# A two-layer MHA + S4D kernel on one core: block 30's sums by a product, a pool for the first-stage buffers, tied additions, a load told to the plan, end additions on VectorE

## The chip, the cores and the metric

The kernel runs on 1 core of one Trainium2 chip. TensorE is PE in the profile, VectorE DVE, ScalarE ACT, GpSimd POOL, SyncE SP; PEld is TensorE's weight load. The metric is the device time of one execution in microseconds, lower is better. Before the change it is 2667.18 us, the median of 3 runs between 2666.62 and 2667.36.

## The reference

A sequence x of 2048 rows and 640 channels passes through two layers, each of them an attention block and then an S4D convolution, each added to x:

```python
def _A_ref(x, wqkv, wo):                      # 32 heads of 20 channels
    ...
    scores = jnp.einsum("bhqd,bhkd->bhqk", q, k) * (Dh ** -0.5)
    p = _softmax(scores, axis=-1)
    o = jnp.einsum("bhqk,bhkd->bhqd", p, v)
    ...
def _B_ref(u, log_A_real, A_imag, C_real, C_imag, log_dt, D_skip):
    ...
    P = jnp.exp((A * dt[:, None])[:, :, None] * pos[None, None, :])
    K = 2.0 * jnp.einsum("dn,dnl->dl", C, P).real      # 128 states a channel
    Kf = jnp.fft.rfft(K, L2)
    Uf = jnp.fft.rfft(u_t, L2)
    y = jnp.fft.irfft(Uf * Kf[None, :, :], L2)[:, :, :L]
    ...
    return y + u * D_skip[None, None, :]
x = x + _A_ref(_layernorm(x, axis=-1), A_wqkv, A_wo)
x = x + _B_ref(_layernorm(x, axis=-1), B_log_A_real, ...)
x = x + _A_ref(_layernorm(x, axis=-1), A_wqkv, A_wo)
x = x + _B_ref(_layernorm(x, axis=-1), B_log_A_real, ...)
```

## The kernel before

**Stages.** In microseconds of the span: layer norm and first projections (0 to 116), attention 1 (to 1093), out-projection 1 with the transform of the S4D kernel (to 1272), S4D convolution 1 (to 1417), layer norm and projections of layer 2 (to 1486), attention 2 (to 2464), out-projection 2 (to 2509), convolution 2 (to the end).

**Attention** (`attention`). 32 blocks, each of 4 heads and 512 queries, run over 16 key tiles. `scores` multiplies S into PSUM (L866) and ACT exponentiates it into pt; `values` multiplies pt with V into pa (L900). V carries a column of ones, so pa also holds each query's sum. At the end of a block DVE adds the two halves of pa into oc, and the sums have to be inverted and spread over the 20 rows of their head. Two ways exist. The usual one goes through DRAM, each step appended to the list `later` with a due time: `sums` and `load` (dn, dr), `invert`, `back`, `spread` (db), and `scale`, which multiplies oc by db (L940) when the next block ends; all these DMAs are issued by POOL. The other, `at_once` (L882), is used for the last block alone: a product of oc with the constant matrix dsel puts each head's sum on all its rows (L886), then DVE does a maximum, a reciprocal and a multiply, and `store_block` stores oc. In layer 1 dsel is the tile late[0], which `prefetch` loads in the step `small` (L1183).

**What fills attention.** PE and DVE have other work laid between the exps: the projections of later heads (`jobs`, `qk`, the matmuls at L618 into PSUM tile m, evicted by DVE into qc) and in attention 1 the generator of the S4D kernel. That generator takes its powers from DRAM (`load_powers`, tile kpw, issued by POOL), and `expand` (L268) multiplies and copies them on DVE into tables, which `contract` multiplies on PE.

**The plan.** The order of each engine's instructions is written out when the program is built. `Plan` (L48) keeps an estimate of the time that PE, ACT and DVE have reached; each DVE operation adds to plan.dve (L80). Filler steps and the entries of `later` are laid where their due time lies by that estimate, and `emptied` lays evictions by it. `tie` (L93) makes an instruction stay behind another on the same engine without a semaphore. Operations of DVE, ACT, POOL and SP are recorded by a helper, so they all show line L78; they are told apart by their tiles.

**End of attention 1.** `prefetch` opens a pool on the memory that the generator has left, loads wo in five pieces (wot, split by POOL into woh and wol) and appends the loads of x, of the first S4D kernel block (kl) and of small tables. Blocks 30 and 31 are the last two (NBK is 32).

**Out-projection 1 and kernel transform.** `out_proj` multiplies po; after each 7th of its matmuls one step of `ktransform` is laid. For each of 5 channel blocks: `by_time` adds the skip weight to the first column of kl (L1250), transposes kl on PE (pkt) and evicts it as ktrh (ACT) and ktrl (DVE); `first_stage` multiplies it with the table e1s into pkx, evicted as x1; `turned` transposes that (pkt again) and evicts it as kxt, by ACT and DVE in turn (L1280); `ends` multiplies pkf, evicted as kn and stored into DRAM as kha and khb. The addition for block 0 is tied behind late[1], those of blocks 1 to 4 are not tied.

**Convolution** (`ssm`, L1385). 40 products of 128x512 (8 of each of 5 channel blocks). `stage1` multiplies the normalised rows uh, ul with e1s (psx, 2 buffers of x1, cast by ACT, rest by DVE); `stage2a` transposes and `sets` multiplies psx; `product` (L1459) shuffles psx on DVE into t, multiplies ka by psx on DVE, kb by t and adds the two on POOL (L1467) for all products but numbers 37 and 39, whose last two steps are on DVE; `stage3` multiplies the result with fa (psv), `stage4` with eb (psy), and DVE adds psy to x. The buffers: s1 (L1408) holds eb, ka, t2 and xt, s2 x1 and v. A pool's tiles may start only when every earlier tile on the same bytes has been released.

Of the kernel before, what the change touches and what calls it, by code (L numbers as in the profile page):

```python
# [87 lines left out]
def mha_s4d_kernel(ctx, tc, x_in, wqkv, wo, lar, aim, cr, ci, ldt, dsk,  # L88
# [109 lines left out]
    def kgen():  # L198
# [69 lines left out]
        def expand(k, w, tab, dif):  # L268

            while slow and slow[0][0] <= k:  # L270
                slow.pop(0)[1]()
            bs = slice(k * BC, k * BC + BC)
            lo = [tab[:, r, :, 0:24].rearrange("p d (g k) -> p d g k", k=8) for r in range(2)]
            hi = [tab[:, r, :, 24:28] for r in range(2)]
            for r in range(2):
                ve.tensor_mul(w[:, r], w[:, r], w[:, 2])
                a3 = w[:, r, 0:9, :].rearrange("p (g k) d -> p d g k", k=3)
                ve.tensor_copy(lo[r][:, :, :, 1:3], a3[:, :, :, 0:2])
                ve.tensor_copy(lo[r][:, :, :, 4:5], a3[:, :, :, 2:3])
                ve.tensor_copy(hi[r][:, :, 0:1], ld["ci" if r else "cr"][:, bs].unsqueeze(2))  # L280
                yield
            cm = [ld[n][:, bs].unsqueeze(2).to_broadcast([P, BC, 3]) for n in ("cr", "ci")]
            yield from cmul([a[:, :, 1:4] for a in hi], [w[:, r, 9:12, :].rearrange("p n d -> p d n") for r in range(2)], cm, [P, BC, 3], "kwc")
            yield from cmul([a[:, :, :, 3] for a in lo], [a[:, :, :, 1] for a in lo],
                            [a[:, :, :, 2] for a in lo], [P, BC, 3], "kwc")
            w4 = [a[:, :, :, 4:5].to_broadcast([P, BC, 3, 3]) for a in lo]
            yield from cmul([a[:, :, :, 5:8] for a in lo], [a[:, :, :, 1:4] for a in lo], w4, [P, BC, 3, 3], "kwb")
            ve.tensor_add(tab[:, 2], tab[:, 0], tab[:, 1])
            yield
            ve.tensor_sub(dif, lo[1][:, :, 0:3:2], lo[0][:, :, 0:3:2])  # L290
# [139 lines left out]
    def attention(x, stats):  # L430
# [461 lines left out]
        def values(qb, g, kt, pts, pa):  # L892
# [10 lines left out]
            if kt == NI - 1:  # L903
# [8 lines left out]
                sums_[0] = plan.dve + 0.15  # L912
                while scaled:
                    scaled.pop(0)()
                if blk == NBK - 1:
                    later.append((plan.dve, lambda: at_once(oc, blk)))
                    return

                def sums():
# [237 lines left out]
    def prefetch(x, rest):  # L1157
# [16 lines left out]
        if rest:  # L1174
# [2 lines left out]
                      *(w1.tile([P, NI, P], F16, name=f"ktr{n}") for n in "hl"),  # L1177
                      *(w1.tile([P, 4, 4, P], F32, name=f"kxt{n}") for n in range(2))]
            late[:] = [w1.tile([P, P], F32, name="dsel")]

            def small():
                sy.dma_start(kl0[1], dsk)
                sy.dma_start(late[0], c_dn)  # L1183
                sy.dma_start(kl0[2], c_f2.rearrange("p (s m) -> p s m", s=2))
            rest[1:1] = small, lambda: load_kl(0)
            with tc.tile_pool(name="wos", bufs=NCT, side="right") as ws:
# [54 lines left out]
    def ktransform(e1):  # L1241

        c = ExitStack()
        c2 = c.enter_context(tc.tile_pool(name="f2", bufs=2))
        kl, skip, f2, x1, hi, lo, *xts = kl0

        def by_time(b, h):

            if h == 0:
                tie(ve.tensor_add(kl[:, 0:1], kl[:, 0:1], skip[:, b:b + 1]), None if b else late[1])  # L1250
            klv = kl.rearrange("d (p i) -> d i p", i=NI)
            for i4 in (2 * h, 2 * h + 1):
                pt = pst("X", [P, 4, P], F32, tag="X", name="pkt")
# [18 lines left out]
        def block(b):  # L1272

            def turned(t, xt, h):
                for q in (2 * h, 2 * h + 1):
# [1 line left out]
                    for g in range(4):  # L1277
                        transpose(pt[:, g, :], of_group(x1, 16 * t + 4 * q + g), ident)
                    if q % 2:
                        ve.tensor_scalar_mul(xt[:, q], pt, ksc[:, 1:2])  # L1280
                    else:
                        se.activation(xt[:, q], pt, AF.Copy, scale=ksc[:, 1:2])

# [103 lines left out]
    def ssm(x, uh, ul, consts, last):  # L1387
# [18 lines left out]
        e1, f2, id16, fa = consts  # L1406
        with ExitStack() as c:
            c1 = c.enter_context(tc.tile_pool(name="s1", bufs=1))  # L1408
            c2 = c.enter_context(tc.tile_pool(name="s2", bufs=2))
            c3 = c.enter_context(tc.tile_pool(name="s3", bufs=3))  # L1410
            order = {}
# [38 lines left out]
                return px  # L1450

            def factors(m, ch):
                ka = c1.tile([P, 512], F32, bufs=5, name="ka")
                kb = c3.tile([P, 512], F32, name="kb")
                for t, src in ((ka, kha), (kb, khb)):
                    at("sp", sy.dma_start(t.rearrange("p (q k) -> p q k", k=P), src[m][:, ch]))
                return ka, kb

            def product(px, ka, kb, alone):  # L1459
                t2 = c1.tile([P, 512], F32, name="t2")  # L1460
                at("dve", ve.stream_shuffle(t2, px, SWAP))
                at("dve", ve.tensor_mul(ka, px, ka))
                for f, *a in (("tensor_mul", kb, t2, kb), ("tensor_add", ka, ka, kb)):
                    if alone:
                        at("dve", getattr(ve, f)(*a))
                    else:
                        at("pool", getattr(ge, f)(*a))  # L1467
                return ka

            def stage3(v, t, ch, t1):  # L1470
# [28 lines left out]
                return add, after  # L1499

            def new_x1():
                return [c2.tile([P, 4, NI // 2, 4, 32], F16, name=f"x1{k}") for k in range(2)]

            x1 = new_x1()
            for i2 in range(8):
                stage1(0, x1, i2)()
            ks, t1s, vs = {}, {}, {}
            NQ = 8 * NCT
            nxt, px = None, None
            sums = None  # L1510
            for n in range(NQ + 15):
# [3 lines left out]
                if n < NQ:  # L1515
                    if q == 0 and b:
                        x1 = nxt
                    if n % 4 == 0:
                        xt = c1.tile([P, 2, 4, 4, P], F16, name="xt")
                    stage2a(x1, q, xt)  # L1520
                if 2 <= n < NQ + 2:
                    ks[n - 2] = factors(*divmod(n - 2, 4))
                if sums:
                    sums[0]()
                if 4 <= n < NQ + 4:
                    t1s[n - 4] = product(px[n % 4], *ks.pop(n - 4), n > NQ and n % 2 == 1)
                if n < NQ and b + 1 < NCT:
                    if q == 0:
                        nxt = new_x1()
# [251 lines left out]
```

## Time and profile before

| | us |
|---|---|
| median of 3 runs | 2667.18 |
| profiled execution | 2665.94 |
| its span (first to last instruction) | 2664.1 |
| PE busy in the span | 2492.7 |
| ACT busy | 2342.6 |
| DVE busy | 1517.5 |
| POOL busy | 813.9 |
| mean granted TensorE clock | 0.993 |

A row of the instruction view shows the start in us from the span's beginning, the duration in us, engine, line, operation, the tile written and the tiles read, partitions x elements and type, and how many instructions like it followed each other. In brackets stand the idle time of that engine just before the row and what ended it: a tile written by another engine, or a DMA. A row whose second column is followed by DMA, or by an engine and a tile without an operation, is of the chain of waits that ended last: start, duration, what ran.

### The profile page before, as it was taken

The numbers are of one execution on the slowest core, as the hardware profiler recorded it, in microseconds if no ns is written. First come the engines' busy times: TensorE is split into PE (matmuls) and PEld (weight loads), VectorE is DVE, ScalarE is ACT, GpSimd is POOL, SyncE is SP. The second block draws the span as 40 slices with busy tenths as digits, with TensorE's granted clock in tenths as the row PEclk, the third lists the DMA queues.
The fourth block names the chain that finished last, engine by engine and source line by source line (L and its number), as shares of the span: only waits on it lengthen the run. The fifth ranks groups of instructions, "written<-read, shape, count | busy, mean of one in ns | idle before, by whom it ended". The sixth has DMA issues, their size and how long they took to land.

```text
span 2664.1 us, 118804 instructions
## 1 busy us (share of the span) xinstructions
PE 2492.7 (94%) x52388; PEld 1408.8 (53%) x52388; DVE 1517.5 (57%) x3417; ACT 2342.6 (88%) x2763; POOL 813.9 (31%) x1240
## 2 busy tenths in 40 slices
PE   7899999999999998799898999999999998999898
PEld 3445445444454443587796444454444443444798
DVE  7687778778855885376787333232232222143875
ACT  7899999999999999565765799999999999999474
POOL 1123334233332332311581122222222223222285
PEclk9999999999999999999999999999999999999999
DMA  6523222222222222454652121121121113222366
GB/s 208 185 52 85 60 78 71 77 57 74 56 60 51 51 69 76 168 204 164 213 175 72 41 58 51 50 60 47 43 67 38 51 32 91 69 67 57 124 201 183
DMA packets 186270, 241.99 MB, mean 91 GB/s; under 512 B 43408, under 2 KB 128720, under 8 KB 184080
## 3 DMA queue, kind: packets, MB, share of 16 engines
q1 hardware_dynamic: 150048, 188.28, 22.5%
q0 software_dynamic: 35696, 46.01, 7.4%
q8 instruction: 413, 6.77, 1.1%
q14 instruction: 113, 0.93, 0.1%
HBM read 158.16 MB, written 76.00 MB: 88 GB/s over the span
## 4 chain that ended last, share of the span: by engine, by line
ACT 58%; PE 19%; issue 10%; DVE 4%; DMA 4%; POOL 1%; SPq 0%; ACTq 0%; POOLq 0%; DVEq 0%
ACT pt L78 56%; PE psy L1417 3%; PE psv L1417 2%; PE pa L900 2%; PE po L193 2%; PE psx L1417 2%; PE S L866 1%; PE pst L1439 1%; PE pkx L193 1%; PE pkt L196 1%; PE m L618 1%; PE pq L771 1%; DVE x L78 1%; PE pkf L193 1%; DMA kl<-kd 0%
## 5 line engine op out<-in xcount | busy, mean ns | idle before, releaser
L78 ACT ACTIVATE pt<-S 128x1024 f32<-128x1024 f32 x2048 | 1927.3, 1033 | 32.9 <-PE S L866 20.3
L900 PE MATMUL pa<-pt,V 64*32 64x512 f32 x16384 | 1095.1, 590 | 0.2 <-DVE oc L78 0.2
L866 PE MATMUL S<-qop,kop 61*32 61x512 f16 x16384 | 874.7, 381 | 85.3 <-ACT pt L78 67.5
L866 PEld LDWEIGHTS <-kop 61*32 61x32 f16 x16384 | 365.8, 89 | 739.3 <-issue 620.1
L900 PEld LDWEIGHTS pa<-pt,V 64*32 64x32 f32 x16384 | 312.3, 106 | 68.6 <-issue 7.9
L78 POOL DMA_DIRECT2D dn<-oc x248 | 122.5, 501 | 595.3 <-DVE oc L78 575.8
L78 DVE TENSOR_SCALAR qc<-m 128x512 f32<-128x512 f32 (+1 forms) x68 | 46.8, 689 | 288.9 <-PE m L618 288.9
L78 POOL DMA_DIRECT2D db<-dn x248 | 125.1, 511 | 139.4 <-DMA dn<-dr 136.5
L78 DVE COPY oc<-pa 128x512 f32<-128x512 f32 x64 | 44.2, 691 | 195.1 <-PE pa L900 184.1
L78 POOL DMA_DIRECT2D ot<-oc x256 | 130.4, 516 | 81.2 <-DVE oc L78 53.8
L618 PE MATMUL m<-xh,wh 64*32 64x512 f16 x2560 | 144.4, 377 | 4.1 <-DVE qc L78 4.1
L618 PE MATMUL m<-xh,wl 64*32 64x512 f16 x2560 | 144.9, 377 | 0.0
L618 PE MATMUL m<-xl,wh 64*32 64x512 f16 x2560 | 143.5, 376 | 0.0
L78 ACT COPY xt<-pst 128x1024 f16<-128x1024 f16 x80 | 81.3, 1016 | 60.8 <-PE pst L1439 60.8
L618 PEld LDWEIGHTS <-wh 64*32 64x32 f16 x5120 | 90.4, 93 | 77.2 <-issue 34.6
L78 POOL DMA_DIRECT2D dn<-dr x62 | 34.5, 557 | 301.8 <-DVE dr L78 274.4
L1467 POOL TENSOR_TENSOR kb<-t,kb 128x512 f32<-128x512 f32 x76 | 97.2, 1279 | 66.8 <-DVE t L78 42.5
L78 DVE TENSOR_SCALAR V<-m 128x160 f32<-128x160 f32 x64 | 20.7, 324 | 161.8 <-PE m L584 161.8
L78 DVE TENSOR_TENSOR kb<-ktab 128x512 f32<-128x512 f32 x160 | 106.1, 682 | 0.0
L584 PEld LDWEIGHTS <-xh 128*128 128x128 f16 x960 | 79.4, 98 | 46.1 <-issue 30.3
L335 PEld LDWEIGHTS m<-kb,ka 128*32 128x32 f32 x3840 | 61.2, 110 | 74.1 <-issue 56.5
L1467 POOL TENSOR_TENSOR ka<-ka,kb 128x512 f32<-128x512 f32 x76 | 97.5, 1283 | 6.0
(312 smaller groups left out, 3945.1 us busy)
## 6 DMA issues: line engine op xcount, KB each, us to landing
ka<-kha SPq DMA_DIRECT2D x80, 256.0 KB
kb<-khb SPq DMA_DIRECT2D x80, 256.0 KB
db<-dn POOLq DMA_DIRECT2D x248, 64.0 KB, 3.3
kop<-ks SPq DMA_DIRECT2D x176, 80.0 KB
kpw<-wd POOLq DMA_DIRECT2D x60, 192.0 KB, 4.4
qop<-qs SPq DMA_DIRECT2D x256, 40.0 KB
ot<-oc POOLq DMA_DIRECT2D x256, 40.0 KB, 2.9
kha<-kn SPq DMA_DIRECT2D x20, 512.0 KB
```

Of the source, the lines that this page charges most:

```text
L78: made = f(out, *a, **k)
L193: chain(te.matmul(*a, **k))
L196: chain(te.transpose(*a, **k))
L335: chain(te.matmul(ps[32 * j:32 * j + 32, c8, :], a[n][:, ch, :], b[n][:, dd, :], start=(n == 0), stop=(n == 2), tile_position=(0, 32 * j)))
L584: chain(te.matmul(ps[:, :n], a_[:, ct, sl], m[:, ct, :], start=(k == 0), stop=(k == 14)))
L618: chain(te.matmul(ps[r][32 * t:32 * t + 32, :], a_[rows, ct, 32 * u:32 * u + 32], m[rows, ct, 512 * v:512 * v + 512], start=(k == 0), stop ...
L771: te.matmul(pq, a_[:, ct, :], m[:, ct, sl], start=(n == 0), stop=(n == 14))
L866: chain(te.matmul(S[32 * t:32 * t + 32, 512 * r:512 * r + 512], kt_[rows, kc + 32 * t:kc + 32 * t + 32], qt[rows, :], start=True, stop=Tru ...
L900: chain(te.matmul(pa[r][32 * j:32 * j + 32, :], V[rows, kt, VP * h:VP * h + 32], pts[j // 2][rows, 512 * (j % 2):512 * (j % 2) + 512], sta ...
L1417: at("pe", te.matmul(*a, **k))
L1439: at("pe", te.transpose(pt[:, k, g, :], of_group(x1[k], 4 * q + g), id16))
L1467: at("pool", getattr(ge, f)(*a))
```

## The change

It has five parts.

1. After the first multiply of the first expansion, plan.dve is raised by 6.0 us.
2. In layer 1 block 30 goes the way of block 31: its `at_once` is appended to `later` with a due time 6.0 us behind the block's end, and `later` is sorted. The load of dsel moves from `small` to the place where the tile is made, ahead of the loads of wo.
3. The addition of the skip weight is tied, for each channel block, behind the last eviction on DVE that `turned` has made (for the first block, as before, behind late[1]).
4. In the convolution x1 has a pool of its own, sx with 2 buffers, behind eb's; ka, t2 and xt move to a pool s4 behind that.
5. The last four products multiply kb on POOL and add on DVE, and each such addition is laid on DVE behind the shuffle and the multiply of the next product. Before, numbers 37 and 39 had both steps on DVE, 36 and 38 both on POOL.

```diff
--- before.py
+++ after.py
@@ -274,6 +274,8 @@
             hi = [tab[:, r, :, 24:28] for r in range(2)]
             for r in range(2):
                 ve.tensor_mul(w[:, r], w[:, r], w[:, 2])
+                if k == r == 0:
+                    plan.dve += 6.0
                 a3 = w[:, r, 0:9, :].rearrange("p (g k) d -> p d g k", k=3)
                 ve.tensor_copy(lo[r][:, :, :, 1:3], a3[:, :, :, 0:2])
                 ve.tensor_copy(lo[r][:, :, :, 4:5], a3[:, :, :, 2:3])
@@ -912,8 +914,9 @@
                 sums_[0] = plan.dve + 0.15
                 while scaled:
                     scaled.pop(0)()
-                if blk == NBK - 1:
-                    later.append((plan.dve, lambda: at_once(oc, blk)))
+                if blk == NBK - 1 or first_layer and blk == NBK - 2:
+                    later.append((plan.dve + (0.0 if blk == NBK - 1 else 6.0), lambda: at_once(oc, blk)))
+                    later.sort(key=lambda e: e[0])
                     return
 
                 def sums():
@@ -1177,10 +1180,10 @@
                       *(w1.tile([P, NI, P], F16, name=f"ktr{n}") for n in "hl"),
                       *(w1.tile([P, 4, 4, P], F32, name=f"kxt{n}") for n in range(2))]
             late[:] = [w1.tile([P, P], F32, name="dsel")]
+            sy.dma_start(late[0], c_dn)
 
             def small():
                 sy.dma_start(kl0[1], dsk)
-                sy.dma_start(late[0], c_dn)
                 sy.dma_start(kl0[2], c_f2.rearrange("p (s m) -> p s m", s=2))
             rest[1:1] = small, lambda: load_kl(0)
             with tc.tile_pool(name="wos", bufs=NCT, side="right") as ws:
@@ -1243,11 +1246,12 @@
         c = ExitStack()
         c2 = c.enter_context(tc.tile_pool(name="f2", bufs=2))
         kl, skip, f2, x1, hi, lo, *xts = kl0
+        hold = [late[1]]
 
         def by_time(b, h):
 
             if h == 0:
-                tie(ve.tensor_add(kl[:, 0:1], kl[:, 0:1], skip[:, b:b + 1]), None if b else late[1])
+                tie(ve.tensor_add(kl[:, 0:1], kl[:, 0:1], skip[:, b:b + 1]), hold[0])
             klv = kl.rearrange("d (p i) -> d i p", i=NI)
             for i4 in (2 * h, 2 * h + 1):
                 pt = pst("X", [P, 4, P], F32, tag="X", name="pkt")
@@ -1277,7 +1281,7 @@
                     for g in range(4):
                         transpose(pt[:, g, :], of_group(x1, 16 * t + 4 * q + g), ident)
                     if q % 2:
-                        ve.tensor_scalar_mul(xt[:, q], pt, ksc[:, 1:2])
+                        hold[0] = ve.tensor_scalar_mul(xt[:, q], pt, ksc[:, 1:2]).ins
                     else:
                         se.activation(xt[:, q], pt, AF.Copy, scale=ksc[:, 1:2])
 
@@ -1406,6 +1410,8 @@
         e1, f2, id16, fa = consts
         with ExitStack() as c:
             c1 = c.enter_context(tc.tile_pool(name="s1", bufs=1))
+            cx = c.enter_context(tc.tile_pool(name="sx", bufs=2))
+            c4 = c.enter_context(tc.tile_pool(name="s4", bufs=1))
             c2 = c.enter_context(tc.tile_pool(name="s2", bufs=2))
             c3 = c.enter_context(tc.tile_pool(name="s3", bufs=3))
             order = {}
@@ -1450,21 +1456,23 @@
                 return px
 
             def factors(m, ch):
-                ka = c1.tile([P, 512], F32, bufs=5, name="ka")
+                ka = c4.tile([P, 512], F32, bufs=5, name="ka")
                 kb = c3.tile([P, 512], F32, name="kb")
                 for t, src in ((ka, kha), (kb, khb)):
                     at("sp", sy.dma_start(t.rearrange("p (q k) -> p q k", k=P), src[m][:, ch]))
                 return ka, kb
 
             def product(px, ka, kb, alone):
-                t2 = c1.tile([P, 512], F32, name="t2")
+                t2 = c4.tile([P, 512], F32, name="t2")
                 at("dve", ve.stream_shuffle(t2, px, SWAP))
                 at("dve", ve.tensor_mul(ka, px, ka))
-                for f, *a in (("tensor_mul", kb, t2, kb), ("tensor_add", ka, ka, kb)):
-                    if alone:
-                        at("dve", getattr(ve, f)(*a))
-                    else:
-                        at("pool", getattr(ge, f)(*a))
+                at("pool", ge.tensor_mul(kb, t2, kb))
+                while adds:
+                    at("dve", ve.tensor_add(*adds.pop(0)))
+                if alone:
+                    adds.append((ka, ka, kb))
+                else:
+                    at("pool", ge.tensor_add(ka, ka, kb))
                 return ka
 
             def stage3(v, t, ch, t1):
@@ -1499,12 +1507,12 @@
                 return add, after
 
             def new_x1():
-                return [c2.tile([P, 4, NI // 2, 4, 32], F16, name=f"x1{k}") for k in range(2)]
+                return [cx.tile([P, 4, NI // 2, 4, 32], F16, name=f"x1{k}") for k in range(2)]
 
             x1 = new_x1()
             for i2 in range(8):
                 stage1(0, x1, i2)()
-            ks, t1s, vs = {}, {}, {}
+            ks, t1s, vs, adds = {}, {}, {}, []
             NQ = 8 * NCT
             nxt, px = None, None
             sums = None
@@ -1516,14 +1524,16 @@
                     if q == 0 and b:
                         x1 = nxt
                     if n % 4 == 0:
-                        xt = c1.tile([P, 2, 4, 4, P], F16, name="xt")
+                        xt = c4.tile([P, 2, 4, 4, P], F16, name="xt")
                     stage2a(x1, q, xt)
                 if 2 <= n < NQ + 2:
                     ks[n - 2] = factors(*divmod(n - 2, 4))
                 if sums:
                     sums[0]()
                 if 4 <= n < NQ + 4:
-                    t1s[n - 4] = product(px[n % 4], *ks.pop(n - 4), n > NQ and n % 2 == 1)
+                    t1s[n - 4] = product(px[n % 4], *ks.pop(n - 4), n >= NQ)
+                    if n == NQ + 3:
+                        at("dve", ve.tensor_add(*adds.pop(0)))
                 if n < NQ and b + 1 < NCT:
                     if q == 0:
                         nxt = new_x1()
```

## Prediction

> **What bounds the kernel now.** I read the page first, then busy times by stretch, then the instructions around the places that the diff touches.
>
> ```profile
> span 2664.1 us, 118804 instructions
> PE 2492.7 (94%) x52388; PEld 1408.8 (53%) x52388; DVE 1517.5 (57%) x3417; ACT 2342.6 (88%) x2763; POOL 813.9 (31%) x1240
> 360.00:1045.00 685.00, 656.86 (x17008) 312.94 (x17014) 519.77 (x1124) 676.93 (x721) 226.51 (x388) 1.00 0.25 62
> 1045.00:1110.00 65.00, 46.54 (x864) 21.37 (x848) 13.16 (x17) 50.32 (x57) 24.32 (x34) 0.95 0.58 198
> 1110.00:1280.00 170.00, 158.09 (x1891) 131.95 (x1892) 122.69 (x274) 94.70 (x158) 23.00 (x19) 0.98 0.49 175
> ```
>
> In the stretch rows the columns are length, then busy time of PE, PEld, DVE, ACT, POOL, granted clock, DMA share, GB/s. In attention 1 (360 to 1045) ACT works 676.9 of 685.0 us: its exps set the pace, and DVE has 165 us to spare. From 1045 to 1110, where attention gives way to the out-projection, nothing is full: PE 46.5 of 65, ACT 50.3, DVE 13.2. The out-projection with the kernel transform (1110 to 1280) is PE's, 158.1 of 170. So an edit pays only where ACT (attention) or PE (elsewhere) stands still. The profiled execution took 2665.94, 1.84 us more than its span and 1.24 under the median of 2667.18; I sum against 2665.94 and carry the difference to the median.
>
> **The plan's load (behind line 276): −5.5 us.**
>
> ```profile
> 123.54 0.56 DVE L78 TENSOR_TENSOR kpw<-kpw 128x384 f32<-128x384 f32 x1 [6.63 <-DMA kpw<-wd]
> 127.11 0.49 PE L618 MATMUL m<-xh,wl 64*32 64x512 f16 x8
> 133.99 0.68 DVE L78 TENSOR_SCALAR qc<-m 128x512 f32<-128x512 f32 x1
> 134.72 0.37 PE L618 MATMUL m<-xh,wh 64*32 64x512 f16 x1 [3.64 <-DVE qc L78]
> 137.43 1.02 ACT L78 ACTIVATE pt<-S 128x1024 f32<-128x1024 f32 x1 [5.13 <-PE S L866]
> 139.46 6.65 ACT L78 ACTIVATE pt<-S 128x1024 f32<-128x1024 f32 x7 [1.01 <-PE S L866]
> ```
>
> DVE waits 6.63 us for the first powers' load, works through their expansion (124.1 to 134.0, 9.9 us), and only then evicts the projection that PE had multiplied at 127.6. PE idles 3.64 us behind it, ACT 5.13 and then 1.01. The 6.0 us tell the plan of that wait, so it should lay the eviction behind at most half of the expansion: 124.1 + 9.9/2 = 129, five us earlier than now, more than PE's 3.64. The expansion that slides behind lies in DVE's spare time; without that cover its 9.9 us would be paid. But the plan's count shifts everything laid after it, so that another eviction can come late: bounds 0 and −6.1 (5.13 + 1.01). I take −5.5: the 5.13 and part of the 1.01.
>
> **The sums of block 30 (lines 915 and 1183): −6.5 us.**
>
> ```profile
> 1075.60 2.16 POOL L78 DMA_DIRECT2D dn<-oc  x4
> 1094.73 1.12 PE L886 MATMUL m<-oc,dsel 128*128 128x512 f32 x2 [0.46 <-DVE oc L78]
> 1096.55 1.26 ACT L78 ACTIVATE ktrh<-pkt,ksc 128x512 f16<-128x512 f32 x2
> 1103.61 0.69 DVE L78 TENSOR_TENSOR oc<-oc,db 128x512 f32<-128x512 f32 x1 [8.93 <-DMA db<-dn]
> 1104.22 0.74 DVE L78 SCALAR_TENSOR_TENSOR ktrl<-pkt,ksc,ktrh 128x512 f16<-128x512 f32 x1
> 1105.02 1.12 PE L196 MATMUL pkt<-ident,kl 128*128 128x128 f32 x4 [8.14 <-DVE ktrl L78]
> 1106.14 3.34 DVE L78 RECIPROCAL db<-db 128x512 f32<-128x512 f32 x1
> 1111.56 0.22 PE L193 MATMUL pkx<-ktrh,e1s 128*128 128x128 f16 x1 [2.57 <-DVE ktrl L78]
> 1096.00:1098.00 2.00, 0.87 (x7) 0.61 (x5) 0.00 (x0) 1.81 (x3) 0.76 (x2) 1.00 1.02 434
> 1102.00:1104.00 2.00, 0.00 (x0) 0.00 (x0) 0.39 (x1) 0.00 (x0) 0.00 (x0) 0.50 0.10 20
> ```
>
> Block 30's sums still go through DRAM, its stores issue only at 1075.6, and its inverse comes back behind loads that keep the DMA engines full (share 1.02 at 1096). DVE stands 8.93 us in front of line 940's scaling; queued behind it is ktrl, for which PE waits 8.14, and PE's clock then runs at 0.50 (1102 to 1104). With the product on PE its sums stay on the chip, without dn, dr or db transfers, and ktrl can go once ACT has written ktrh, at 1096.55 plus half of 1.26, so from about 1097.3. That is 1104.22 − 1097.3 = 6.9 us earlier, and pkx moves from 1111.56 to about 1104.7, just behind its e1s table: the DMA share is down to 0.10 at 1102, so the loads had landed by then. In exchange block 30 pays what block 31 pays: 1.12 us of PE, 0.7 max, 3.34 reciprocal, 0.7 multiply. DVE's three, 4.7 us, lie in the 51.8 idle us of 1045 to 1110; without that room the 3.34 would stand in front of block 31's copy of oc, for which the dsel product waits, and be paid. PE's 1.12 mostly fits its gaps between exps: +0.4. The dsel load, one issue of some 0.4 us, moves ahead of wo's on SP. If the loads bind instead, the 8.14 shrinks only by the removed transfers: bounds −2 to −7.5. I take −6.9 + 0.4 = −6.5.
>
> The Trainium skill (TensorE: Matmul & The Clock Gate, The HAM clock gate) says that after a few us of idleness PE is halved and needs about 3.4 us of work to be released. The trace agrees: 0.50 behind the 8.14 us. By it an idle time cut to under 3 us would also speed up the pkt and pkx behind it: some 4 us of work at half clock, an estimate of 2 us, and −8.5 for this part.
>
> **The tied additions (lines 1250 and 1280): −4.0 us.**
>
> ```profile
> 1145.13 0.16 DVE L78 TENSOR_TENSOR kl<-kl,skip 128x1 f32<-128x1 f32 x1 [2.08 <-DMA kl<-kd]
> 1175.81 0.92 DVE L78 TENSOR_TENSOR kl<-kl,skip 128x1 f32<-128x1 f32 x1 [1.14 <-DMA kl<-kd]
> 1209.47 0.16 DVE L78 TENSOR_TENSOR kl<-kl,skip 128x1 f32<-128x1 f32 x1 [3.87 <-DMA kl<-kd]
> 1210.08 0.70 PE L193 MATMUL po<-woh,ol 128*128 128x320 f32 x3 [2.93 <-DVE x L78]
> 1200.00:1220.00 20.00, 16.71 (x196) 13.10 (x195) 11.43 (x27) 8.97 (x16) 2.78 (x2) 0.91 0.63 217
> 1225.83 0.75 DVE L78 TENSOR_SCALAR kxt<-pkt,ksc 128x512 f32<-128x512 f32 x1 [0.43 <-PE pkt L196]
> 1226.82 0.90 PE pkt L196 x8
> ```
>
> DVE blocks on the next block's kl load three times (2.08, 1.14, 3.87); PE feels only the third: 2.93 us idle, and the stretch to 1220 has 3.3 us of idle and a clock of 0.91, which costs 20 × 0.09 = 1.8 more: 5.1. Tied behind the last turned eviction (1225.83 + 0.75 = 1226.6), the addition starts when PE reaches kl's transposes (1226.82), long after the load. Its 0.16 us then stands before PE in each of four blocks: up to +0.2 each, 0.8. Behind it on DVE are the evictions of po, for which PE's next po waits. −5.1 + 0.8 is −4.3; I take −4.0. If the tie makes PE wait for a whole round trip in each block, the bound is the dearest such stall seen, 5.1 each: −5.1 to −5.1 + 20.4 = +15.3.
>
> **Pools (lines 1408, 1454 and 1502): −0.8 us.**
>
> ```profile
> 1274.28 4.39 DMA khb<-kn
> 1275.78 0.56 ACT L78 CAST x<-psx 128x512 f16<-128x512 f32 x1
> 2513.14 0.56 ACT L78 CAST x<-psx 128x512 f16<-128x512 f32 x1
> L1417 PE MATMUL psx<-uhx,e1s x320: 216/219/314, 2474.9 to 2612.2; 128*128 128x128 f16 x160
> 2514.48 0.23 PE L1417 MATMUL psx<-uhx,e1s 128*128 128x128 f16 x1 [4.96 <-DVE va L78]
> ```
>
> A tile waits for every earlier tile that lay on its bytes. In layer 2 the first first-stage product ran at 2474.9, yet its cast at 2513.14: it shared bytes with wo's weights. In a pool of their own the x1 buffers lie on attention's, long free, so casts run beside the out-projection and PE's 4.96 us can go: 0 to −5, and I take −2.5, since the row names the LN's va as what PE waits for last. In layer 1, by tile sizes, the first x1 buffer now overlaps the second half of the transform's kn buffer, whose khb store lands 1274.28 + 4.39 = 1278.67: the cast at 1275.78 waits 2.9 us, and behind it on ACT the evictions that PE's next stage needs. 0 if PE has other work for as long, +3 if not; I take +1.7. Sum −0.8 (bounds −5 to +3).
>
> **Additions at the end (lines 1459–1468 and 1526): +4.0 us.**
>
> ```profile
> 1398.09 1.28 POOL L1467 TENSOR_TENSOR ka<-ka,kb 128x512 f32<-128x512 f32 x1
> 1398.05 0.73 DVE L78 STREAM_SHUFFLE t<-psx 128x512 f32<-128x512 f32 x1
> 1398.68 0.67 DVE L78 TENSOR_TENSOR ka<-psx,ka 128x512 f32<-128x512 f32 x1
> 1399.42 1.16 PE L1417 MATMUL psv<-fa,ka 128*128 128x128 f32 x8
> 1400.19 0.69 DVE L78 TENSOR_TENSOR ka<-ka,kb 128x512 f32<-128x512 f32 x1
> 2488.24 1.47 POOL L1231 TENSOR_TENSOR ulx<-u,uhx 128x640 f16<-128x640 f32 x1 [9.96 <-issue]
> 2488.55 1.18 DVE L78 TENSOR_TENSOR lt<-rs 128x2 f32<-128x2 f32 x1
> ```
>
> Product 36's addition ran on POOL until 1399.37, and psv followed at 1399.42. Now it runs on DVE behind the next shuffle and multiply: those end at 1399.35, plus 0.69, so psv starts at 1400.05: +0.6, for which I allow 0.9 in layer 2. Unblocked: +1.5. But a DVE operation on two SBUF tiles beside a POOL one can take longer: a 2-column lt took 1.18 us, to the end of POOL's ulx (2489.71), where the 1-column kl above took 0.16. So the addition would wait for POOL's multiply of product 37, which now follows the shuffle: 1398.78 + 1.28 = 1400.06, psv at 1400.75: +1.33, and with product 38's shuffle queued behind it, for which POOL waits in turn, about 0.5 for each of the next two: 2.4 a layer, +4.8. I take +4.0, near the blocked end.
>
> The Trainium skill (SBUF — State Buffer, Who interferes with whom) has it as a lock: a DVE instruction with two SBUF inputs waits out a GpSimd instruction that reads SBUF. It speaks against this edit. The trace agrees by the 1.18 us; by it the sum would be +4.8, without it +1.5.
>
> **Sum.** −5.5 − 6.5 − 4.0 − 0.8 + 4.0 = −12.8. The profiled execution goes to 2653.1, the median to 2667.18 − 12.8 = 2654.4.
>
> **Rivals.**
> 1. The plan's load only moves the stall: its count is wrong by as much elsewhere, another eviction meets another load. For it: DVE's order is fixed by an estimate of a load that took 6.63 us; against: DVE has room. −12.8 + 5.5 = −7.3: 2659.9.
> 2. The passage at 1100 is bound by loads, since the DMA engines are full from 1096 on. For: share 1.02; against: 0.10 at 1102, so the loads were over while DVE still waited. The sums' part falls from −6.5 to −2: 2658.9.
> 3. Slower: the tied addition becomes PE's wait. PE's order is chained; the addition follows the turned eviction, kl's transposes follow the addition, and PE has nothing laid between. From a round trip of about 3 us on, when the clock drops too, each of four blocks pays 5.1: the tie's −4.0 becomes +15.3, the sum −8.8 + 15.3 = +6.5, so 2673.7. Against: 0.16 us of addition, and only one eviction ahead.
> 4. The additions run unblocked, since the lt row is a single one (+1.5 for +4.0), and layer 2's casts save all 5 (−5 for −2.5): −12.8 − 5.0 = −17.8, so 2649.4. For: POOL and DVE share no row of this kind at the ends; against: the 1.18 ends when ulx does.
> 5. The change doesn't do what it says: the list of due times or the ties leave the order as it is. Nothing gained, nothing lost: 2667.
>
> **How the numbers follow.** Chances: forecast 0.47, rival 1 0.13, rival 2 0.12, rival 3 0.08, rival 4 0.12, rival 5 0.08. The likeliest case's own range is 2648 to 2660. The range 2644 to 2665 takes in rivals 1, 2 and 4 and most bounds (all at their low ends: −6.1 − 7.5 − 5.1 − 5 + 1.5 = −22.2, or 2645.0); rivals 3 and 5 are outside. A measurement of this kernel can tell 0.2%, 5.3 us: no change is 2661.8 to 2672.5. Faster: 0.46 of the forecast, 0.10 each of rivals 1 and 2, 0.12 of rival 4: 0.78. Same: 0.01, 0.03, 0.02 and 0.06 of these and rival 5: 0.12. Slower: rival 3 and 0.02 of rival 5: 0.10.
>
> **What would show it.** Plan: the exp wait of 5.13 us near 137 gone, and none of its size new before 400. Sums: no db wait over 2 us at 1095 to 1104, no half-clock stretch there, PE's 8.14 under 2. Tie: no kl wait on DVE, the stretch around 1200 to 1220 at clock 1.00; wrong if pkt waits for kl in every block. Pools: casts before 2500 in layer 2, a first cast after 1278 in shifted time in layer 1. Additions: psv waits for DVE instead of POOL at the ends, additions of 0.69 against up to 1.3 us. The forecast as a whole is wrong if the exps of attention lengthen, or a new wait of over 5 us on PE or ACT shows up in another place.

## The result and the profile after

The changed kernel takes 2674.44 us (median of 16 runs) against 2667.27 of the kernel before (16 runs): ratio 1.0027, interval 1.0019 to 1.0035. It is 7.2 us slower, where 12.8 less was forecast. The profiled execution took 2673.31, 1.13 under its median; its span is 2671.5, against 2664.1.

To see where it went, I took the same instruction (the n-th of its kind) in both traces, counted from 0. The last column is what the stretch above it added.

| instruction | before | after | lead (−) or lag | added |
|---|---|---|---|---|
| exp 0 | 116.03 | 114.60 | −1.43 | ahead of the change |
| exp 64 | 182.67 | 175.87 | −6.80 | −5.4 |
| exp 320 | 428.68 | 417.45 | −11.23 | −4.4 |
| exp 960 | 1032.81 | 1026.90 | −5.91 | +5.3 |
| first x += po | 1115.62 | 1116.60 | +0.98 | +6.9 |
| x += po 28 | 1257.84 | 1258.18 | +0.34 | −0.6 |
| first t of convolution 1 | 1290.95 | 1295.62 | +4.66 | +4.3 |
| x += psy 32 | 1410.89 | 1417.36 | +6.47 | +1.8 |
| exp 1984 | 2400.24 | 2408.33 | +8.09 | +1.6 |
| first t of convolution 2 | 2531.06 | 2537.95 | +6.89 | −1.2 |
| x += psy 72 | 2651.42 | 2658.77 | +7.35 | +0.5 |

The start gains what was forecast. Instruction rows of DVE in the changed kernel, with the columns as in the prediction:

```profile
122.03 0.56 DVE L78 TENSOR_TENSOR kpw<-kpw 128x384 f32<-128x384 f32 x1 [6.58 <-DMA kpw<-wd]
...
127.41 0.69 DVE L78 TENSOR_SCALAR qc<-m 128x512 f32<-128x512 f32 x1 [2.08 <-PE m L620]
```

The wait for the powers is still there (6.58), but the eviction now follows the product of PE (it waits for m, 2.08) and runs at 127.41 instead of 133.99. Then the end of attention 1. First the rows of POOL, SP and ACT, before:

```profile
1046.57 0.93 POOL L78 DMA_DIRECT2D kd<-ko  x1 [5.88 <-issue]
...
1074.10 1.55 POOL L1191 TENSOR_TENSOR wol<-wot,woh 128x640 fp32r<-128x640 f32 x1
1075.68 0.38 SPq L78 DMA_DIRECT2D otl<-ot  x1
1095.91 0.73 ACT L78 CAST oh<-otl 128x640 fp32r<-128x640 f32 x1 [3.87 <-DMA otl<-ot]
```

and after, with the rows of DVE, PE and ACT that follow from them:

```profile
1055.76 0.94 POOL L78 DMA_DIRECT2D kd<-ko  x1 [8.70 <-DVE ko L78]
...
1059.34 0.37 SPq L78 DMA_DIRECT2D dsel<-in_c_dn  x1
1060.06 2.27 SPq L78 DMA_DIRECT2D wot<-in_wo  x5
1061.30 2.05 PE L888 MATMUL m<-oc,dsel 128*128 128x512 f32 x2 [2.24 <-DMA dsel<-in_c_dn]
1064.04 1.02 ACT L78 ACTIVATE pt<-S 128x1024 f32<-128x1024 f32 x1 [3.61 <-PE S L868]
1073.75 3.05 POOL L1194 TENSOR_TENSOR wol<-wot,woh 128x640 fp32r<-128x640 f32 x2 [8.86 <-issue]
1082.52 1.55 POOL L1194 TENSOR_TENSOR wol<-wot,woh 128x640 fp32r<-128x640 f32 x1
1084.10 0.38 SPq L78 DMA_DIRECT2D otl<-ot  x1
1104.19 0.72 ACT L78 CAST oh<-otl 128x640 fp32r<-128x640 f32 x1 [13.78 <-DMA otl<-ot]
1105.54 0.75 DVE L78 SCALAR_TENSOR_TENSOR ktrl<-pkt,ksc,ktrh 128x512 f16<-128x512 f32 x1 [10.88 <-ACT ktrh L78]
1106.35 1.12 PE L196 MATMUL pkt<-ident,kl 128*128 128x128 f32 x4 [7.98 <-DVE ktrl L78]
```

This is one chain. The S4D generator stores its last piece (kd) and frees its memory; wo is loaded there, POOL splits it, and only when the last wol is written can otl be loaded into what wot leaves. In both kernels otl goes out within 0.1 us of POOL's end (1074.10 + 1.55 = 1075.65, 1082.52 + 1.55 = 1084.07) and reaches ACT 20.2 and 20.1 us later (1095.91, 1104.19). Attention is 5.9 us earlier than before, but the generator ends 9.2 us later. So DVE no longer waits 8.93 us for db but 10.88 for ktrh, and PE's idle time is 7.98 where it was 8.14. The product for block 30 itself found dsel not landed and stopped PE for 2.24 us and the exps for 3.61.

The places of the other three parts, in rows of the changed kernel:

```profile
1128.21 1.03 PE L196 MATMUL pkt<-ident,kl 128*128 128x128 f32 x7 [0.32 <-issue]
1161.41 0.80 PE L196 MATMUL pkt<-ident,kl 128*128 128x128 f32 x5 [0.34 <-ACT oh L78]
1192.99 1.14 PE L196 MATMUL pkt<-ident,kl 128*128 128x128 f32 x8 [0.86 <-issue]
1238.19 1.90 PE L196 MATMUL pkt<-ident,kl 128*128 128x128 f32 x8 [2.27 <-ACT kxt L78]
...
1280.30 2.05 ACT L78 CAST x<-psx 128x512 f16<-128x512 f32 x4 [3.33 <-DMA khb<-kn]
1281.66 0.27 PE L1423 MATMUL psx<-uh,e1s 128*128 128x128 f16 x1 [6.22 <-DVE x L78]
1281.72 0.31 PE L1423 MATMUL psx<-ul,e1s 128*128 128x128 f16 x1
...
1403.65 1.27 POOL L1469 TENSOR_TENSOR kb<-t,kb 128x512 f32<-128x512 f32 x1 [0.85 <-DVE t L78]
1404.05 1.41 DVE L78 TENSOR_TENSOR ka<-ka,kb 128x512 f32<-128x512 f32 x1
1405.72 1.13 PE L1423 MATMUL psv<-fa,ka 128*128 128x128 f32 x8 [1.52 <-DVE ka L78]
...
2484.73 0.58 ACT L78 CAST x<-psx 128x512 f16<-128x512 f32 x1
2523.56 0.27 PE L1423 MATMUL psx<-uhx,e1s 128*128 128x128 f16 x1 [4.81 <-DVE x L78]
```

Two of these places in the kernel before:

```profile
1239.42 1.17 PE L196 MATMUL pkt<-ident,kl 128*128 128x128 f32 x8 [2.27 <-ACT kxt L78]
...
1277.12 0.22 PE L1417 MATMUL psx<-uh,e1s 128*128 128x128 f16 x1 [2.02 <-DVE x L78]
```

PE stops in front of kl's transposes in blocks 1, 2 and 3; the 2.27 us of block 4 are there in both kernels. ACT's first cast of convolution 1 waits 3.33 us for the last store of khb, and PE idles 6.22 us instead of 2.02. Then a psx matmul takes 0.31 us, at a granted clock of 0.50 (1281 to 1285). The Trainium skill (TensorE: Matmul & The Clock Gate, The HAM clock gate) says that PE's clock halves when it stands still for a few us; these rows agree. The slow clock is no difference between the two kernels, though: before, it fell to 0.54 at 1279 to 1281, and the lag is 4.5 us at the first cast already and 4.7 at the first t. The addition on DVE takes 1.41 us instead of 0.69 beside POOL's multiply. In layer 2 the first cast moved from 2513.14 to 2484.73, but PE's wait at the start of the convolution is 4.81 us, against 4.96 before.

### The profile page after: what moved, and what is told of

It is laid out like the page before. It is cut to its first block, busy times and chain, and to the rows that moved or that the text cites. A ratio compares the mean times of both kernels' runs of the same rounds, so it can differ in the third digit from the quotient of the medians.

```text
span 2671.5 us, 118774 instructions
## 1 busy us (share of the span) xinstructions
PE 2499.0 (94%) x52390; PEld 1411.4 (53%) x52390; DVE 1520.2 (57%) x3417; ACT 2344.5 (88%) x2763; POOL 805.7 (30%) x1230
## 5 line engine op out<-in xcount | busy, mean ns | idle before, releaser
L78 ACT ACTIVATE pt<-S 128x1024 f32<-128x1024 f32 x2048 | 1928.3, 1033 | 32.6 <-PE S L868 20.2
L1423 PE MATMUL psv<-fa,ka 128*128 128x128 f32 x640 | 89.1, 282 | 7.2 <-DVE ka L78 5.7
```

Of the source, the lines that this page charges most:

```text
L78: made = f(out, *a, **k)
L1423: at("pe", te.matmul(*a, **k))
```

## The experiments

My theory after this: the 6 us told to the plan make the generator late, and its end gates the passage; in layer 1 the new pool, and at the ends the new order, cost more than they save. The rivals are given with each run. The kernel before was timed beside each group; it lay between 2665.5 and 2667.1 us.

**Without the plan's load.**

```diff
                 ve.tensor_mul(w[:, r], w[:, r], w[:, 2])
-                if k == r == 0:
-                    plan.dve += 6.0
```

> The changed kernel without the plan's 6 us; the other four parts stay. Theory (the 6 us make the generator of the S4D kernel late: its last store goes out at exp 992 instead of 975, and the loads of wo, kl, otl and e1s wait for the memory that it frees): the last store is back at exp 975, dsel and wo are issued near 1050, ACT's wait for otl near 1093 shrinks from 13.8 to under 5 us, ktrl runs near 1097.3 instead of 1104.2, and block 30's product finds dsel landed. Sum against the kernel before: start 0, passage -6.5, tied additions -0.6, pools +4.3 and -1.3, additions at the ends +2.3: -1.8 us, ratio 0.9993. Rival (the passage is bound by the loads' volume, whenever they start): ktrl stays near 1104, the sum is +4 to +5 us.

Measured: 2669.20 us, ratio 1.0011 (1.0000 to 1.0023). As expected the generator's last store is back at exp 975 and its passage gains: from exp 896 to the first x += po the lead over the kernel before grows from 1.79 to 5.97 us. But the whole is 2.9 us slower than before, not 1.8 faster. In its trace the pools took 4.8 of the lead (6.66 to 1.91), the end of convolution 1 another 1.8 (to 0.16), and the end of convolution 2 1.8 (+7.25 to +9.07), somewhat more than I had put down. In attention 2, which this edit leaves alone, the profiled execution, 5.8 us above its median, lost 8.0 us (+0.41 to +8.42). PE's waits for loads of qop and kop there are 6.0 us instead of 3.8. Of the 8.0 us 5.5 fall between exps 1792 and 1856: PE waits 2.06 and 0.74 us for qop at 2250, the granted clock is 0.56 and 0.58 in the two stretches of 4 us from 2252 on, and ACT stands still for 5.2 us in all.

**The plan's load alone.**

```diff
                 ve.tensor_mul(w[:, r], w[:, r], w[:, 2])
+                if k == r == 0:
+                    plan.dve += 6.0
```

> The kernel before with the plan's 6 us alone. Theory (late generator): 5.5 to 6 us earlier up to the end of attention 1, then ACT waits over 12 us for otl and ktrh runs near 1104, so that nothing is left of the lead: +0.5 to +1.5 us against the kernel before, ratio about 1.0004. Rival (the 6 us and the passage have nothing to do with each other; the passage is spoilt by block 30's product): -5.5 us, ratio 0.9979.

Measured: 2674.45 us, ratio 1.0029 (1.0017 to 1.0042): 7.7 us slower. The rival falls; the loss is larger than the theory's. ACT, in this kernel:

```profile
1105.39 0.72 ACT L78 CAST oh<-otl 128x640 fp32r<-128x640 f32 x1 [17.74 <-DMA otl<-ot]
```

From exp 960 to the first x += po it goes from 4.44 us ahead to 9.67 behind: 14.1. The changed kernel lost 6.9 there. So here the late generator costs about 14 us, and in the changed kernel the sums of block 30 had given 7 of them back.

**The sums of block 30 alone.**

```diff
-                if blk == NBK - 1:
-                    later.append((plan.dve, lambda: at_once(oc, blk)))
+                if blk == NBK - 1 or first_layer and blk == NBK - 2:
+                    later.append((plan.dve + (0.0 if blk == NBK - 1 else 6.0), lambda: at_once(oc, blk)))
+                    later.sort(key=lambda e: e[0])
...
+            sy.dma_start(late[0], c_dn)
...
-                sy.dma_start(late[0], c_dn)
```

> The kernel before with block 30's sums by a product, and the moved dsel load, alone. Theory (late generator spoilt this part): dsel lands before block 30 ends, no 2.2 us wait of PE, DVE's wait for db is gone, ktrl near 1097.3, and the rest of the kernel is 6.5 us earlier: ratio 0.9976. Rival (loads' volume binds): at most -2 us, ratio 0.9993 or above; second rival (the product in front of block 31 costs more than it saves): slower than before.

Measured: 2660.07 us, ratio 0.9978 (0.9968 to 0.9987): 6.2 us faster. SP, DVE and PE in this kernel:

```profile
1047.77 0.37 SPq L78 DMA_DIRECT2D dsel<-in_c_dn  x1
...
1096.73 0.75 DVE L78 SCALAR_TENSOR_TENSOR ktrl<-pkt,ksc,ktrh 128x512 f16<-128x512 f32 x1 [3.10 <-ACT ktrh L78]
...
1097.54 0.72 PE L196 MATMUL pkt<-ident,kl 128*128 128x128 f32 x4 [1.70 <-DVE ktrl L78]
```

dsel's load is issued 15.6 us before its first use, ktrl runs at 1096.73 (forecast: 1097.3), and PE's idle time is 1.70 instead of 8.14. Both rivals fall. By the trace the passage itself gives 4.2 us (lead 3.28 at exp 896, 7.46 at the first x += po); the rest of its profiled lead was there at exp 64 already (3.24), ahead of any edit. So the trace shows less than the 6.2 us of the medians, whose interval reaches from 3.5 to 8.5.

**A smaller load on the plan.**

```diff
-                    plan.dve += 6.0
+                    plan.dve += 2.0
```

> The changed kernel with 2.0 us told to the plan instead of 6.0. In the built order the generator then ends at exp 969, as before the change (973), while only the last three operations of the first expansion, some 2 us, move behind the eviction. Theory (late generator): -2 us at the start, passage as in the kernel without the plan's load, -6.5, rest +4.7: -3.8 us against the kernel before, ratio 0.9986. Rival (any load on the plan spoils the passage): as the changed kernel, +3 to +7 us.

Measured: 2654.54 us, ratio 0.9956 (0.9940 to 0.9973): 11.8 us faster than before, with all five parts in. The rival falls; the gain is three times what I expected. By the trace 7.7 us are won between exp 0 and exp 320, where I expected 2, and 7.8 between exp 960 and the first x += po. The generator's last store goes out at 1035.2, 11 us earlier than before, and ACT's idle time in front of its cast of otl is 0.95 instead of 3.87.

**A late generator without the first expansion's load.**

```diff
                 ve.tensor_mul(w[:, r], w[:, r], w[:, 2])
+                if r == 0 and k == 10:
+                    plan.dve += 20.0
```

beside the sums of block 30 as above, nothing else.

> The kernel before with block 30's sums by a product (as sums_alone), and with 20 us told to the plan at the eleventh expansion instead of 6 at the first one. The start is then as in the kernel before, and in the built order the generator ends at exp 989 instead of 973. Theory (the generator's end gates the passage): start not faster, the loads of dsel and wo go out some 13 us later, ACT waits over 8 us for otl, and most of the 6.2 us that sums_alone gained are gone: +3 to +8 us against the kernel before. Rival (what spoilt the passage was something at the first expansion): as sums_alone, 2660.

Measured: 2671.92 us, ratio 1.0022 (1.0011 to 1.0033): 5.9 us slower than before, where the same kernel without these two lines is 6.2 faster. SP and ACT:

```profile
1061.33 0.37 SPq L78 DMA_DIRECT2D dsel<-in_c_dn  x1
...
1106.87 0.72 ACT L78 CAST oh<-otl 128x640 fp32r<-128x640 f32 x1 [15.57 <-DMA otl<-ot]
```

dsel goes out 13.6 us later than in sums_alone, and otl keeps ACT waiting for 15.57 us. The first expansion is laid as before the change; what moved is the generator, from its eleventh piece on. So a late end alone is enough.

**The new pool in layer 2 only.** On top of plan_2us:

```diff
-                return [cx.tile([P, 4, NI // 2, 4, 32], F16, name=f"x1{k}") for k in range(2)]
+                return [(cx if last else c2).tile([P, 4, NI // 2, 4, 32], F16, name=f"x1{k}") for k in range(2)]
```

> The changed kernel with 2.0 us told to the plan (as plan_2us), and with x1 in its old pool s2 in layer 1, in the new pool sx in layer 2 only. Theory (in layer 1 the first x1 buffer waits for the stores of khb, and PE idles 6.2 us at the start of the first convolution instead of 2.0): ACT's first cast no longer waits for khb, PE's idle there is back at 2.0, and all that follows is 4.3 us earlier than in plan_2us, while layer 2 keeps its early casts: about 2650.2 us, ratio 0.9940. Rival (the cast is late for another reason, the order of ACT): no change against plan_2us, 0.9956.

Measured: 2649.88 us, ratio 0.9950 (0.9933 to 0.9966). ACT and PE:

```profile
1256.66 0.56 ACT L78 CAST x<-psx 128x512 f16<-128x512 f32 x1
...
1258.01 0.22 PE L1423 MATMUL psx<-uh,e1s 128*128 128x128 f16 x1 [2.03 <-DVE x L78]
```

The wait for khb is gone, PE's idle time is back at 2.03, and against plan_2us the first cast is 4.2 us further ahead than the x += po just before it (7.23 against 3.05). The rival falls. The intervals of the two ratios overlap; it is the traces that tell the kernels apart.

**The additions ahead of the next shuffle.** On top of plan_2us:

```diff
             def product(px, ka, kb, alone):
                 t2 = c4.tile([P, 512], F32, name="t2")
+                while adds:
+                    at("dve", ve.tensor_add(*adds.pop(0)))
                 at("dve", ve.stream_shuffle(t2, px, SWAP))
                 at("dve", ve.tensor_mul(ka, px, ka))
                 at("pool", ge.tensor_mul(kb, t2, kb))
-                while adds:
-                    at("dve", ve.tensor_add(*adds.pop(0)))
```

> As plan_2us, but each deferred addition of the last four products is laid on DVE ahead of the next product's shuffle instead of behind its multiply, so that POOL has no operation to run beside it. Theory (DVE's addition of two SBUF tiles stands still while POOL multiplies): the additions take 0.69 us instead of 1.41, psv of products 36 to 38 waits under 0.7 us instead of 1.25 to 1.52, and each layer's end is 1 to 2 us shorter: 2651 to 2653 us. Rival (an addition takes 1.41 us for a reason of its own): rows of 1.41 stay, and the end is as long as in plan_2us.

Measured: 2653.08 us, ratio 0.9957 (0.9944 to 0.9970). Additions on DVE and multiplies on POOL, first in plan_2us, then here:

```profile
1387.88 1.41 DVE L78 TENSOR_TENSOR ka<-ka,kb 128x512 f32<-128x512 f32 x1
...
1387.47 1.27 POOL L1469 TENSOR_TENSOR kb<-t,kb 128x512 f32<-128x512 f32 x1 [0.85 <-DVE t L78]
```

```profile
1385.71 0.69 DVE L78 TENSOR_TENSOR ka<-ka,kb 128x512 f32<-128x512 f32 x1
...
1387.14 1.27 POOL L1471 TENSOR_TENSOR kb<-t,kb 128x512 f32<-128x512 f32 x1 [1.46 <-DVE t L78]
```

Each of the eight additions takes 0.69 us, and no psv waits over 0.3 us any more. The Trainium skill (SBUF — State Buffer, Who interferes with whom) describes the lock between a DVE instruction with two SBUF inputs and a GpSimd one that reads SBUF; these rows agree, and 1.41 against 0.69 is its price here. By the traces the end of layer 1 is 1.6 us shorter than in plan_2us, that of layer 2 1.2. The medians, 1.5 us apart, cannot tell it. In the profiled execution, 2.4 us above its median, a wait in attention 2 gave 3.5 us back.

**The tie behind the first turned step.** On top of plan_2us:

```diff
-                        hold[0] = ve.tensor_scalar_mul(xt[:, q], pt, ksc[:, 1:2]).ins
+                        made = ve.tensor_scalar_mul(xt[:, q], pt, ksc[:, 1:2]).ins
+                        if q == 1:
+                            hold[0] = made
```

> As plan_2us, but the addition to kl is tied behind the first eviction on DVE of the block's first turned step (the eviction of q = 1) instead of the last one. Theory (tied behind the last one it stands right in front of PE's transposes of kl): the waits of 0.3, 0.3 and 0.9 us ahead of the kl transposes of blocks 1 to 3 go, the one of 2.3 us of block 4 goes or shrinks to under 1, and the third block's stall stays away: 1.5 to 3.5 us faster than plan_2us, 2651 to 2653. Rival (PE waits there for the evictions of kxt, not for the addition): all these waits stay.

Measured: 2654.43 us, ratio 0.9957 (0.9943 to 0.9971), no change that the times could tell. In the trace the waits in front of kl's transposes in blocks 1 to 3 are gone and 2.2 us with them (from 0.17 behind plan_2us at the first ktrh to 2.07 ahead at ACT's kxt 16). In block 4 the rival was right:

```profile
1219.75 1.97 PE L196 MATMUL pkt<-ident,kl 128*128 128x128 f32 x8 [2.27 <-ACT kxt L78]
```

This wait is 2.27 us in plan_2us and in the kernel before too: it is for the eviction of kxt, and the tie has no part in it.

**All corrections together**, then the same with the last products as before the change, with 6.0 us on the plan, and with none.

```diff
-                    plan.dve += 2.0
+                    plan.dve += 6.0
```

is the edit of fixed_6us; fixed_0us drops the line and its condition, adds_before takes product and its call from the kernel before.

> All five parts, each with what the runs so far say: 2.0 us told to the plan, block 30's sums by a product, the additions to kl tied behind the first turned eviction, x1 in its own pool in layer 2 only, the deferred additions ahead of the next shuffle. Theory (the four corrections act in separate stages and add up): plan_2us less 4.2 (first casts), 2.2 (kl transposes) and 2.5 to 3 (ends of both layers): 2645 to 2646 us, ratio 0.9920. Rival (what is saved in one stage is waited for in the next): 2649 or above, not below the kernel pools_last.

> As best2, but the last four products as in the kernel before (numbers 36 and 38 wholly on POOL, 37 and 39 on DVE). Theory: the early additions save about 0.6 us of POOL per product against before, so this one is 0 to 2 us slower than best2: 2646 to 2648. Rival (moving the additions to DVE is no gain in any order): equal to best2 or faster.

> As best2, but with the 6.0 us of the changed kernel told to the plan. Theory (the 6 us alone make the generator end late, whatever the other parts do): the generator's last store at exp 992, ACT waits over 10 us for otl, and the kernel is 15 to 20 us slower than best2, 2661 to 2666 us, ratio 0.998 to 1.000. Rival (the late passage came from the other parts as well): under 10 us slower.

> As best2, but nothing told to the plan (the order of the start as in the kernel before). Theory (2 us on the plan save some 2 us at the first eviction and the 3 to 4 us stall near 367, and move the generator's end 4 exps ahead): 4 to 6 us slower than best2, 2646 to 2648. Rival (the start's gain is lost again within attention): equal to best2 within 2 us.

| kernel | us | ratio to before | interval |
|---|---|---|---|
| best2 | 2642.08 | 0.9910 | 0.9895 to 0.9925 |
| adds_before | 2644.94 | 0.9911 | 0.9896 to 0.9926 |
| fixed_6us | 2660.92 | 0.9978 | 0.9968 to 0.9989 |
| fixed_0us | 2659.41 | 0.9978 | 0.9967 to 0.9989 |

best2 beats both kernels: 25.0 us faster than the one before in the same group. The corrections add up, so its rival falls. It is 3 us faster than the 2645 expected; in its profile the clock stays at 1.00 behind block 4's wait, where it fell in plan_2us, which by the traces makes 1.5 us. Whether the additions belong on DVE (best2) or on POOL (adds_before) stays open: 2.9 us between the medians, equal ratios, so the rival of adds_before is not ruled out. With 6.0 us on the plan the last store of the generator is back at exp 992, ACT waits 15.95 us for otl, and 18.8 us are lost, as the theory had it. With nothing on the plan I expected 4 to 6 us more than best2; it is 17.3 by the medians and 18 by the ratios. ACT's wait for otl, first in fixed_0us, then the same cast in best2:

```profile
1097.04 0.73 ACT L78 CAST oh<-otl 128x640 fp32r<-128x640 f32 x1 [3.66 <-DMA otl<-ot]
```

```profile
1083.64 0.72 ACT L78 CAST oh<-otl 128x640 fp32r<-128x640 f32 x1
```

At exp 896 fixed_0us is 8.0 us behind best2, at the first x += po 12.7. So once db no longer comes later, the generator's end is on the path even where it lies as in the kernel before: otl keeps ACT waiting for these 3.7 us, and the 2 us on the plan, which bring the end forward from 1046.6 to 1033.1, take nearly all of them out. At the end of convolution 1 it is 14.1 behind. The rest lies in attention 2, where this profile, 5.6 us above its median, shows 7.6 us of PE's waits for qop and kop against 2.9 in best2; nearly all of the 6.8 us that it loses there fall at two places, around exps 1297 and 1825.

## Why the prediction was wrong

**The plan's load** was forecast at −5.5 and gave −5.4 at exp 64: eviction, product and exps moved as described. Up to exp 320 it gave 4.4 more, which the forecast did not have. In the kernel before, ACT waits in front of exps 257 to 259:

```profile
367.49 1.02 ACT L78 ACTIVATE pt<-S 128x1024 f32<-128x1024 f32 x1 [3.04 <-PE S L866]
369.06 1.02 ACT L78 ACTIVATE pt<-S 128x1024 f32<-128x1024 f32 x1 [0.55 <-PE S L866]
370.87 1.94 ACT L78 ACTIVATE pt<-S 128x1024 f32<-128x1024 f32 x2 [0.79 <-PE S L866]
```

After the change the first of these waits is 0.67 us and the others are gone. The step that failed is the sentence "The expansion that slides behind lies in DVE's spare time". DVE's busy share was the wrong measure. The plan lays generator steps only while its count of DVE is not ahead of PE, so the load delayed the whole generator: each of its stores comes at least 17 exps later, from the first one (exp 79 instead of 60) to the last (992 instead of 975), and from exp 0 to that last store DVE stands idle for 233 us, 12 more than before. And the generator's end opens the memory for the loads that the passage waits for. From exp 960 to the first x += po the price is 14 us in plan_alone, 11 in late_generator against sums_alone, and 17 in fixed_6us against best2. Rival 1's moved stall came too, behind the 400 us up to which it was looked for: between exps 384 and 416 (from 477 us on) the three kernels with 6.0 us on the plan lose 2.6 to 3.6 us, those with 2.0 us under 0.1. It is the smaller part.

**The sums of block 30** were right in mechanism and about right in size: −6.5 forecast, −6.2 alone by the medians, 4.2 to 5.2 in the trace of the passage, by where one starts to count. In the changed kernel they were swallowed, because db was only the last of two things that DVE stood in front of. The forecast took ACT's ktrh, at 1096.55, as fixed and saw that the DMA share fell at 1102. In front of ktrh ACT waits for otl, 3.87 us already before the change, and that wait took over when the generator's end moved: ktrl runs at 1105.54, where 1097.3 was forecast.

**The tied additions** were forecast at −4.0 and gave −0.6. Block 3's stall went, as described: it gave −4.0 (forecast: −5.1), and as much in each tied kernel; the clock from 1200 to 1220 is 1.00 after, 0.91 before. "Up to +0.2 each" was mis-sized: the three waits are 0.32, 0.34 and 0.86, and up to block 3 the lag grows by 1.7 (forecast: 0.8). Another +1.6 comes behind block 4's wait of 2.27 us, which the forecast didn't have: there the clock is 0.57 in the next 4 us, and 1.00 in the kernel before, though the wait is the same. It fell in eight of the ten profiled kernels with the ties and in none of the four without them; why isn't shown. Rival 3 was this mechanism at 5.1 us a block; it is real at 0.3 to 0.9. Its sum of 2673.7 lies close to what was measured, but by coincidence. best2, tied behind the first turned eviction and without the slow clock, gains 4.4 us in this stretch.

**The pools** were forecast at −0.8 and gave +4.3 − 1.2 = +3.1. The overlap with khb's store was read rightly, but "I take +1.7" was too small: the store landed later than before (1280.3 against 1278.67) and PE had nothing else, so idle time went from 2.02 to 6.22, past the bound of +3. Layer 2 gave half of the −2.5, and not by the step named: PE's 4.96 us stayed (4.81, now for x instead of va); what went are two waits of 0.55 and 0.53 us behind it.

**The additions at the ends** were forecast at +4.0 and gave +1.8 + 0.5 in this pair of traces (1.8 + 1.8 in no_plan); the mechanism (waiting for POOL's multiply) was right, as adds_early shows.

By the table the plan's load and the sums together gave −5.4 − 4.4 + 5.3 + 6.9 = +2.4 instead of −12.0, the pools +3.1, the additions +2.3, the tie −0.6. With 1.6 in the layer norm and attention 2, which no edit touches, and −1.4 ahead of the change this is the profile's +7.4.

## What to carry to other kernels

An engine that is three quarters busy hides moved work only if the work's end gates nothing: ask what memory it frees, which load waits for that memory, and how long that load takes to reach the engine that sets the end. In a kernel whose order is laid by an estimate, a number added to the estimate acts on everything laid behind it; compare the built orders for several values (here 2.0 and 6.0) before taking one. And when a stall is removed, look for the next operand of the same instruction that is just behind.

## What the runs showed that I had not expected

The plan's answer to the load is a step: with 2.0 us the generator ends at exp 971, with 6.0 at 992 (975 before), and 4 us of plan are worth 18.8 us of time.

POOL's first wol starts 8.76 us (before), 8.86 (after), 8.41 (sums_alone) and 10.13 us (late_generator) after POOL's last work, and the profile names no releaser but issue. That lies on the chain from the generator to otl. What causes it wasn't tried.

PE's waits for loads of qop and kop in attention 2, which none of these edits touches, sum to 2.4 to 7.6 us in the profiled executions. In no_plan one such wait of 2.8 us cost ACT 5.2, with the slow clock behind it. Much of the spread of some 10 us between runs of one kernel may come from there; only one execution of each kernel was traced.
